# A planned attention-and-FFN kernel: filler matmuls in any free bank, a new identity and first-load order, v on VectorE only, SyncE holds in the planner, and a new instruction order

## The chip, the cores and the metric

The kernel runs on one core of a Trainium2 chip. The metric is the device time of one execution in microseconds (us), from the runs' timer. The profile's span runs from the first to the last instruction of one profiled execution; the timer shows a little more, for what lies around it.

## The reference

There are two stages. The first is linear attention with a "hedgehog" feature map, for 8 batches of 8 heads, 576 tokens, head width 64:

```
phi(x)  = [exp(p), exp(-p)]  with p = x @ w_phi - max|x @ w_phi|        (128 + 128 features)
kv      = sum over tokens of phi(k)^T v ;  z = sum over tokens of phi(k)
attn    = (phi(q) @ kv) / (phi(q) . z + 1e-6)
```

The second is a feed-forward network (FFN) on the 4608 tokens, laid out as 4608 x 512: `relu(x @ w_in)^2 @ w_out` with 2048 hidden units. Inputs and output are float32; the kernel's matmuls take bfloat16 and accumulate in float32.

## The kernel before

**Tiling.** A batch of attention has five groups of tokens: groups 0 to 3 hold 128-row blocks of two heads each, and group 4 holds the last 64 tokens of all heads (the "singles", tiles named `xks`, `xqs`, `xvs` below for their loads). For keys: a transpose gives `kT`; `project` (L598) or, in batch 0, L626, makes the projection in PSUM; VectorE takes the maximum (`mk`); ScalarE takes exp with both signs (`kp`, `kn`) and the exp of the maximum (`em_ops`); `v_ops` multiplies v by that factor into `va` (L720 for the singles, L724 for the rest); `kv_ops` (L741, L746) accumulates `kv`. For queries: `qmax_ops` and `q_ops` project twice (L774 or L598 for the maximum, L816 for the features), ScalarE makes `qp` and `qn`, and `out_ops` (L846) multiplies by `kv`, with a VectorE rescale between the two signs (L858), a reciprocal (L866) and the division (L870) into `xo`. `xo` is transposed into `xT`, the FFN's input.

**Transposes.** Batches 0 and 1 (`PE_IN`) transpose k and q on TensorE (L569) and copy the result out of PSUM; lists `CK`, `CQ`, `CK1`, `CQ1` say on VectorE or ScalarE. Batches 2 to 7 use DMA transposes issued by SyncE (SP), L582, one for k and one for q in a batch, each 18 blocks; `xo` goes through SP too from batch 1 on (L908).

**FFN.** The FFN runs in 9 chunks of 512 tokens, one batch behind attention (`ffn_in_small` L1003 for chunk 0, `ffn_in` L992, `ffn_out` L1057, `last_out` L1021), followed by ReLU on ScalarE (L972), the square on VectorE (L978), and stores from three `ot` buffers by SP (L1074). Chunk 8 collects the singles of all batches.

**Loads.** All loads of q, k, v and both weights go through the GpSimd (POOL) queue, cast on the way, at most eight in flight. `w_phi` comes in two halves through SP (L433).

**The order.** It is written out by a planner. `plan.add` records every operation with an engine, a cost (occupancy, latency), a key (due time) and what it reads and writes. `Machine.run` then simulates the engines: an engine that is free takes the available operation with the smallest key, subject to free PSUM banks (`place`, `fit`, `LIM`), and to two modes of TensorE ("tiled" projections with 64-row weights and the rest; a change of mode has a price). Keys are the list `KEYS`; `RELEASES` gives the earliest time of each load from batch 2 on, and `pin` makes such a load wait for the ScalarE instruction that the plan shows as finished by then (its "gate"). Each engine's program is then in plan order, and each engine executes strictly in its order.

**Planned DMA.** The planner has one DMA queue for SP and one for POOL. `SLACK` adds time to a landing by its class ("first" for the first two batches' loads and the weights, "ld" for later loads, "x" for transposes of `xo`, "kq" for those of k and q); `SHARE` is SP's part when both queues have work.

**Filler.** [...] the last loop of the kernel puts matmuls on a tile of zeros (`warm`, L1144) into each planned idle stretch of TensorE before `WARM_UP` = 23 us. They write PSUM bank 7, which the planner keeps free until then. The identity for TensorE's transposes is made on POOL by `make_identity` (a memset, then an `affine_select`), planned behind the first k load.

Of the kernel before, what the change touches and what calls it, by code (L numbers as in the profile page):

```python
# [22 lines left out]
SLACK = {"first": 0.4, "ld": 1.5, "x": 1.5, "kq": 2.5}  # L23
BEGIN = {"POOL": 1.25}
WARM_UP, COLD = 23.0, 6.0
# [14 lines left out]
class Op:  # L40
    __slots__ = ("eng", "occ", "lat", "key", "fn", "opens", "closes", "dma", "tiled", "release", "gate",
                 "succ", "n", "ready", "at", "seq", "what", "ins", "left", "done", "slack")

    def __init__(self, eng, cost, key, fn, opens, closes, dma, tiled, release, seq, what):
        self.eng, (self.occ, self.lat), self.key, self.fn = eng, cost, key, fn
        opens = () if opens is None else opens if isinstance(opens, tuple) else (opens,)
        self.opens, self.closes, self.dma, self.seq, self.what = opens, closes, dma, seq, what
        self.tiled, self.release, self.gate, self.ins = tiled, release, None, None
        self.succ, self.n, self.ready, self.at, self.done = {}, 0, 0.0, None, None
        self.slack = SLACK[dma[3]] if dma is not None and len(dma) > 3 else 0.0  # L50
# [48 lines left out]
class Machine:  # L99
# [5 lines left out]
    SHARE = {"x": 0.36, "st": 0.67, "ld": 0.5}  # L105

    def __init__(self, plan, limits, ahead, patience, want):
        self.plan, self.limits = plan, limits
        self.ahead, self.patience, self.want = ahead, patience, want
        self.free_at = [0.0] * (self.BANKS - 1) + [WARM_UP]  # L110
        self.open = {}
        self.q = {"SP": [], "POOL": []}
        self.q_t, self.q_v = 0.0, 0
        self.hist = {"SP": [], "POOL": []}
# [45 lines left out]
    def dma_advance(self, t):  # L160
        done = []
        while self.q_t < t - 1e-12:
            sp = self.speeds()
            step = t - self.q_t
            for k, l in self.q.items():
                if l:
                    step = min(step, l[0].left / sp[k])
            for k, l in self.q.items():
# [8 lines left out]
    def run(self):  # L177
# [28 lines left out]
        def dma_settle(t):  # L206
# [6 lines left out]
            sp = self.speeds()  # L213
            nxt = [self.q_t + l[0].left / sp[k] for k, l in self.q.items() if l]
            if nxt:
# [36 lines left out]
        while left:  # L252
# [12 lines left out]
            if e["free"] > t + 1e-9:  # L265
# [4 lines left out]
            while e["pending"] and e["pending"][0][0] <= t + 1e-9:  # L270
                bisect.insort(e["avail"], heapq.heappop(e["pending"])[2])
            op = pick(name, e, t)
# [8 lines left out]
            op.at = t  # L281
# [30 lines left out]
            if op.dma is not None:  # L312
                op.left = op.dma[0]
                self.hist[name].append(op)
# [8 lines left out]
def kernel(  # L323
# [107 lines left out]
    def f_wphi(half):  # L431
        def fn():
            pin(nc.sync.dma_start(out=wphi_f[half * 64 : half * 64 + 64, :], in_=w_phi))  # L433
        return fn

    for half in range(2):
        add("SP", (0.6, 0), -10, f_wphi(half), w=[("wphi_f", half)], dma=(0.3, HW_IN, "ld"), what="wphi")
# [8 lines left out]

    warmed = add("DVE", dve_cost(32), -1e4, f_warm, w=["warm"], what="warm")
# [102 lines left out]
    def attention(b):  # L550
# [157 lines left out]
        def v_ops(g0, g1, key):  # L708

            gs = [4] if g0 == 4 else list(range(g0, g1))  # L710
            for sg in range(2):
                on = K["CV"][2 * g0 + sg] if first else "DVE"
                ve = nc.vector if on == "DVE" else nc.gpsimd
                def fn(sg=sg, ve=ve):
                    t = va[s2][sg]
                    if g0 == 4:
# [3 lines left out]
                        pin(ve.tensor_tensor(  # L720
                            out=o[:, :, :, :D], in0=x, in1=o[:, :, :, D].to_broadcast([P, 4, 2, D]), op=ALU.mult))
                    else:
                        o = t[:, 8 * g0 : 8 * g1, :]
                        pin(ve.tensor_tensor(  # L724
# [3 lines left out]
                add(on, dve_cost(n) if on == "DVE" else (n / 500 + 0.1, n / 500 + 0.3), key, fn, r=of("xv", b, ["s"] if g0 == 4 else gs) + [("ve", s2, sg, g) for g in gs],  # L728
# [284 lines left out]
    def last_out(c, tt, part, key):  # L1013
# [26 lines left out]
        for half in range(2):  # L1040
            for u, (name, e) in enumerate((("SP", nc.sync), ("ACT", nc.scalar))):
# [4 lines left out]
                add(name, (0.5, 0.5), key + half, fn, r=[("otl", half)], what="stl")  # L1046
# [33 lines left out]
    def f_ident():  # L1080
        make_identity(nc, ident)

    add("POOL", (0.8, 1.0), -8.9, f_ident, w=["ident"], what="ident")
# [42 lines left out]
    warmed.key = -1e4  # L1126
# [9 lines left out]
    for op in order:  # L1136
        if op.eng == "PE" and op.at < WARM_UP:
            now[0] = filler
            n = 0
            while idle + (0.11 if idle < COLD else 0.058) < op.at - 0.03:  # L1140
                idle += 0.11 if idle < COLD else 0.058
                n += 1
            for _ in range(n):
                pin(nc.tensor.matmul(out=psum[:, 7, :P], lhsT=warm, rhs=warm, start=True, stop=True))  # L1144
# [21 lines left out]
    'CV': ['POOL', 'DVE', 'DVE', 'POOL', 'DVE', 'DVE', 'DVE', 'DVE', 'DVE', 'POOL'],  # L1166
    'KM': [1, 1, 1, 1, 1],
    'CK': ['DVE', 'ACT', 'ACT', 'DVE', 'DVE'],
    'CQ': ['DVE', 'DVE', 'DVE', 'ACT', 'ACT'],
    'CK1': ['ACT', 'ACT', 'ACT', 'ACT', 'DVE'],  # L1170
    'CQ1': ['DVE', 'DVE', 'DVE', 'DVE', 'DVE'],
# [4 lines left out]
    'LIM': {'tp': 6, 'b0': 7, 'att': 3, 'kv': 1, 'op': 2},  # L1176
    'AHEAD': 27.826,
    'PATIENCE': 5.762,
# [4 lines left out]
    -1188, 474, 253, 754, 1267, 528, 1719, 419, -2007, -2938, -2908, -2981, -4303, -4282, -3330, -3499, 919, 649,  # L1183
    1370, 2080, 1937, 1125, 1588, 1758, 2021, 2630, 1260, 2159, 2716, 4112, 2907, -2846, 3771, -1876, 4962, 4961,
    3120, 3409, 24214, 17442, 18795, 44151, 1509, 2174, 657, 972, 5105, 139, 1554, 1343, -8, 2664, 4605, 2242, 2239,
    1135, 1840, 5585, 430, 1295, 2238, 1136, 1707, 1336, 945, 443, 3793, 29611, 29873, 194, -588, 827, 594, 15584,
    776, 166, 14628, 305, 21064, 146, 1125, 885, 2743, 25589, -2180, 107, 907, 23181, 1452, 16457, 3036, 2675, 973,
    35728, 1936, 2335, 1747, 1866, 1305, 1774, 1112, 2112, 2270, 1379, 1304, 26789, 216, 26250, 17049, 1162, 2001,
    1665, 28376, 1869, 2852, 2457, 1250, 935, 1220, 2270, 1616, 1054, 10645, 20672, 2478, 1178, 2010, 999, 1923,
    393, 2483, 11257, 2804, 22023, 2533, 10980, 5031, 2532, 1743, 2463, 2204, 13503, 1506, 2348, 2785, 4142, 2901,  # L1190
    36176, 9646, 3718, 14023, 2255, 2290, 299, -72, 13807, 11062, 2403, 2778, 2102, 17466, 11387, 2050, 2319, 5032,
    14049, 8912, 1855, 14681, 1658, 2595, 25827, 3886, 3958, 10742, 18466, 4286, 7320, 4146, 26325, 2594, 9501,
    2696, 21621, -190, 22614, -1704, 2640, 35906, 4111, 22553, 3566, 6591, -314, 7751, 9572, 5930, 4224, 8630,
    14150, 14672, 4292, 7860, 4443, 2689, 2858, 7055, 3974, 4816, 6018, 2943, 13108, 2777, 2404, 33150, 35566, 3635,
    2965, 3806, 1699, 4189, 15290, 4266, 20860, 3962, 20258, 4549, 5477, 3203, 1892, 3524, 2854, 3813, 4795, 4887,
    4532, 5059, 6753, 20587, 26251, -357, 18509, -87, 3069, 5510, 31932, 1422, 6588, 5358, 6315, 1913, 4618, 24242,
    6773, 5370, 5986, 4151, 34128, 6057, 8183, 15483, 5660, 6078, 29747, 14492, 6266, 15335, 6540, 4409, 4759, -392,
    5661, 5347, 5290, 7491, 5505, 6298, 5763, 5960, 25044, 183, -812, 4467, 4387, 5327, 2497, 6865, 7116, 4719,
    6177, 5627, 6010, 6083, 6121, 6278, 4167, 24496, 7776, 8245, 6597, 6765, 29553, 5314, 11573, -110, 15484, 4913,
    6178, 8838, 19649, -231, 4916, 30701, 7786, 8322, 12085, 35149, 3500, 1077, 5339, 3084, -356, 3451, 3054, 17648,  # L1200
    2824, 2922, 16842, 5248, 3803, 2746, 14132, 5658, 17523, 29471, 5655, 3354, 4095, 4822, 5666, 4427, 5397, 3918,
    6360, 6495, 4759, 18063, 5919, 4532, 4501, 6236, 4423, 37527, 5746, 5835, 6510, 4027, 5065, 26396, 1751, 4806,
    5892, 9033, 5894, 4282, 5468, 5858, 1344, -3520, 3667, 24946, 25273, 25359, 3238, 4543, 4906, -95, 1079, 12985,
    7480, 10129, 2325, 37292, 53, 9165, 7565, 9657, 3425, 20459, 9576, 9725, 8791, 19377, 8125, 19178, 23716, 8786,
    -1952, 7595, 29986, 7634, 18755, 8663, 15981, 12146, 9487, 10448, 8819, 8908, 8691, -1929, 9521, 8863, 21811,
    9570, 10185, 7836, 11282, 9154, 7332, 37424, 7462, 7045, 6935, 6786, 9216, 9235, 19462, 10195, 11284, 8928,
    10835, 8511, 2871, 9295, 9783, 24159, 8664, 11351, 10113, 11142, 22190, 10398, 17777, 3185, 2391, -253, -948,
    11128, -2534, 425, 20649, 32343, 9102, 2944, 8733, 11654, 12476, 10197, 10427, 10530, 9734, 10615, 8748, -1123,
    10681, 6537, 10759, 12413, 12082, 32361, 14465, 3268, 11422, 11238, 11707, 11582, 23355, 12263, 11570, 4035,
    6591, 2840, 5604, 4489, 7936, 8602, 9080, 6114, 2760, 9508, 6016, 9010, 8259, 8506, -421, 6285, 7836, 7574,  # L1210
    8525, 9517, 18673, 7044, 6862, 7853, 13963, 7876, 8335, 5210, 5767, 7599, 8898, 29260, 5554, 5410, 8243, 9334,
    17403, 9243, 24144, 8353, 9108, 30600, 36971, 9137, 6764, 31407, 20905, 8686, 19278, 9290, 7237, 20576, 9945,
    9482, 9050, 10364, 27769, 11167, 8564, 5763, 4446, 10315, 8988, 16403, 4858, 9954, 6527, 11610, 7075, 5392,
    27034, 9410, 5480, -3552, 9698, 20309, 11741, 11397, 8887, 10295, 10825, 37395, 38223, 10882, 12346, 10736,
    9404, 12019, 9290, 228, 10345, 4314, 10319, 9622, 10045, 11538, 23123, 12591, 13084, 9699, 10200, 11107, 14578,
# [103 lines left out]
```

## Time and profile before

| | |
|---|---|
| median of 4 runs | 371.92 us (370.09 to 373.41) |
| the profiled execution's own time | 371.43 us |
| its span | 369.7 us, 8551 instructions |
| TensorE busy, VectorE, ScalarE, GpSimd | 350.4, 254.7, 267.5, 69.6 us |
| mean granted TensorE clock | 0.997 |
| bytes moved by DMA | 39.61 MB, 101478 packets |

How to read it: a matmul of 512 columns shows about 379 ns in the trace, but matmuls are pipelined, and successive ones start 216 ns apart (the starts in the trace). So busy time overstates what TensorE does. Where the text speaks of TensorE work in us, it counts matmuls at the distance of their starts: 216 ns for 512 columns, 56 ns for 128, 29 ns for 65, half of that for a tiled pair with 64-row weights. "Position 43 on TensorE" is a point of the program with 43 us of such work ahead of it; positions are counted in the instruction order as it is written out. In profile lines, a bracket gives the idle time of the engine before an instruction and what ended it; "SPq" and "POOLq" are the sequencers that issue DMAs.

### The profile page before, as it was taken

The numbers are of one execution on the slowest core, as the hardware profiler recorded it, in microseconds if no ns is written. First come the engines' busy times: TensorE is split into PE (matmuls) and PEld (weight loads), VectorE is DVE, ScalarE is ACT, GpSimd is POOL, SyncE is SP. The second block draws the span as 40 slices with busy tenths as digits, with TensorE's granted clock in tenths as the row PEclk, the third lists the DMA queues.
The fourth block names the chain that finished last, engine by engine and source line by source line (L and its number), as shares of the span: only waits on it lengthen the run. The fifth ranks groups of instructions, "written<-read, shape, count | busy, mean of one in ns | idle before, by whom it ended". The sixth has DMA issues, their size and how long they took to land.

```text
span 369.7 us, 8551 instructions
## 1 busy us (share of the span) xinstructions
PE 350.4 (95%) x3494; PEld 198.6 (54%) x3494; DVE 254.7 (69%) x426; ACT 267.5 (72%) x507; POOL 69.6 (19%) x99
## 2 busy tenths in 40 slices
PE   7977899978999999999999999999999999999994
PEld 7956778533564455545555445455454554444452
DVE  3997998768887977895787748888587750531500
ACT  3978998569959698898785977997787753723620
POOL 8795213001213320321003200013000000000000
PEclk9999999999999999999999999999999999999998
DMA  8999997971969798699929993158630032011023
GB/s 111 142 195 199 192 121 95 150 157 25 166 97 131 155 170 117 122 150 145 78 83 162 128 192 99 42 106 94 129 94 28 2 96 76 0 37 57 2 61 81
DMA packets 101478, 39.61 MB, mean 107 GB/s; under 512 B 76096, under 2 KB 96960, under 8 KB 101440
## 3 DMA queue, kind: packets, MB, share of 16 engines
q0 software_dynamic: 50592, 18.36, 46.2%
q1 hardware_dynamic: 50688, 20.59, 25.7%
q8 instruction: 27, 0.44, 0.5%
q10 hardware_dynamic: 160, 0.13, 0.1%
q14 instruction: 11, 0.09, 0.1%
HBM read 36.77 MB, written 9.44 MB: 125 GB/s over the span
## 4 chain that ended last, share of the span: by engine, by line
PE 57%; ACT 18%; DMA 9%; DVE 6%; issue 6%; POOL 2%; POOLq 0%; DVEq 0%; ACTq 0%
PE psum L992 22%; PE psum L1057 22%; ACT hr L972 4%; DMA xT<-xo 4%; PE psum L846 4%; ACT kp L684 3%; ACT kn L684 2%; DMA xk<-in_k_dram 2%; PE psum L741 2%; ACT qp L831 2%; PE psum L598 2%; DVE mq L781 2%; DMA kT<-xk 2%; PE psum L816 1%; ACT ot L1065 1%
## 5 line engine op out<-in xcount | busy, mean ns | idle before, releaser
L1057 PE MATMUL psum<-wout,h 128*128 128x512 bf16 x560 | 133.9, 379 | 0.5 <-ACT ot L1065 0.5
L992 PE MATMUL psum<-xT,win 128*128 128x512 bf16 x448 | 104.3, 379 | 4.5 <-DMA xT<-xo 2.6
L972 ACT ACTIVATE hr<-psum 128x512 bf16<-128x512 f32 x144 | 83.1, 608 | 29.3 <-PE psum L992 19.0
L978 DVE TENSOR_TENSOR h<-hr 128x512 bf16<-128x512 bf16 x144 | 58.9, 419 | 46.2 <-ACT hr L972 44.6
L992 PEld LDWEIGHTS <-win 128*128 128x128 bf16 x512 | 47.6, 98 | 61.1 <-issue 6.2
L1057 PEld LDWEIGHTS <-h 128*128 128x128 bf16 x560 | 50.2, 98 | 53.7 <-issue 2.3
L781 DVE TENSOR_REDUCE mq<-psum 128x8 f32<-128x1024 f32 (+1 forms) x40 | 43.9, 1111 | 9.1 <-PE psum L598 8.8
L831 ACT ACTIVATE qp<-psum 128x1024 bf16<-128x1024 f32 (+1 forms) x40 | 37.6, 944 | 10.0 <-PE psum L816 6.8
L1065 ACT ACTIVATE ot<-psum 128x512 f32<-128x512 f32 x35 | 21.1, 601 | 29.5 <-PE psum L1057 21.2
L724 DVE TENSOR_TENSOR va<-xv,va 128x1024 bf16<-128x1024 bf16 (+1 forms) x34 | 38.6, 1152 | 5.1 <-ACT va L703 5.1
L678 DVE TENSOR_REDUCE mk<-psum 128x8 f32<-128x1024 f32 (+1 forms) x35 | 38.0, 1108 | 3.8 <-PE psum L598 3.4
L858 DVE TENSOR_TENSOR psum<-psum,en 128x520 f32<-128x520 f32 (+1 forms) x40 | 27.6, 702 | 17.2 <-PE psum L846 11.8
L831 ACT ACTIVATE qn<-psum 128x1024 bf16<-128x1024 f32 (+1 forms) x40 | 37.6, 947 | 0.4 <-PE psum L846 0.4
L684 ACT ACTIVATE kp<-psum 128x1024 bf16<-128x1024 f32 (+1 forms) x35 | 32.8, 939 | 6.8 <-DVE mk L678 6.5
L684 ACT ACTIVATE kn<-psum 128x1024 bf16<-128x1024 f32 (+1 forms) x35 | 33.1, 945 | 0.1
L870 DVE TENSOR_TENSOR xo<-psum,rden 128x512 bf16<-128x512 f32 (+1 forms) x40 | 27.2, 685 | 1.0
L487 POOL DMA_DIRECT2D xq<-in_q_dram x16 | 14.2, 888 | 39.9 <-ACT va L703 13.8
L741 PE MATMUL psum<-va,kp 128*128 128x65 bf16 x256 | 19.9, 194 | 0.2 <-ACT kv L756 0.2
L476 POOL DMA_DIRECT2D xk<-in_k_dram x16 | 10.1, 630 | 53.0 <-DVE mq L781 19.7
L741 PE MATMUL psum<-va,kn 128*128 128x65 bf16 x256 | 19.9, 193 | 0.0
L741 PEld LDWEIGHTS <-kp 128*128 128x128 bf16 x256 | 17.4, 97 | 4.0 <-DVE va L724 0.9
L846 PEld LDWEIGHTS <-qp 128*128 128x128 bf16 x320 | 14.3, 97 | 8.9 <-issue 2.3
(67 smaller groups left out, 379.5 us busy)
## 6 DMA issues: line engine op xcount, KB each, us to landing
out_dram<-ot SPq DMA_DIRECT2D x32, 256.0 KB, 2.4
xv<-in_v_dram POOLq DMA_DIRECT2D x8, 512.0 KB, 7.8
xq<-in_q_dram POOLq DMA_DIRECT2D x16, 256.0 KB, 6.4
xk<-in_k_dram POOLq DMA_DIRECT2D x7, 512.0 KB, 7.1
win<-in_moe_w_in_dram POOLq DMA_DIRECT2D x4, 512.0 KB, 8.7
wout<-in_moe_w_out_dram POOLq DMA_DIRECT2D x4, 512.0 KB, 11.4
out_dram<-ot SPq DMA_DIRECT2D x6, 128.0 KB, 2.3
xk<-in_k_dram POOLq DMA_DIRECT2D x16, 32.0 KB, 4.9
```

Of the source, the lines that this page charges most:

```text
L678: pin(nc.vector.tensor_reduce(out=mk_view(g), in_=ps2(pj)[:, :, : n * Fd].rearrange("p e (i f) -> p e i f", f=Fd), axis=AX.X, op=ALU.max, ...
L684: pin(nc.scalar.activation(out=dst[slot][:, :, :n, :].rearrange("p e i f -> p e (i f)"), in_=ps2(pj)[:, :, : n * Fd], func=ACT.Exp, scale= ...
L724: pin(ve.tensor_tensor(out=o[:, :, :D], in0=xv[s2][:, 512 * g0 : 512 * g1].rearrange("p (m d) -> p m d", d=D), in1=o[:, :, D].to_broadcast ...
L741: pin(nc.tensor.matmul(out=o[:, sg, hi, :], lhsT=(kp, kn)[sg][kgroup[pr]][:, j % 2, 2 * hi + j // 2, :], rhs=va[s2][sg_of(sg, pr)][:, 8 * ...
L781: pin(nc.vector.tensor_reduce(out=mqb[:, c, :, :n], in_=ps2(pj)[:, :, : n * Fd].rearrange("p e (i f) -> p e i f", f=Fd), axis=AX.X, op=ALU ...
L831: pin(nc.scalar.activation(out=o, in_=i_, func=ACT.Exp, scale=sgn))
L846: pin(nc.tensor.matmul(out=o[:, u // 4, u % 4 * D1 : (u % 4 + 1) * D1], lhsT=(qp, qn)[sg][slot][:, u * m : u * m + P], rhs=kv_sb[s2][:, h ...
L858: pin(nc.vector.tensor_tensor(out=o, in0=o, in1=enb[:m, c, :].rearrange("t (b h) -> t b h", b=2).to_broadcast([m, 2, 4, D1]), op=ALU.mult))
L972: pin(nc.scalar.activation(out=hr[sl], in_=ps1(g), func=ACT.Relu))
L978: pin(nc.vector.tensor_tensor(out=dst, in0=i_, in1=i_, op=ALU.mult))
L992: pin(nc.tensor.matmul(out=o, lhsT=win[mc // 4][:, kc, mc % 4 * P : (mc % 4 + 1) * P], rhs=x, start=(kc == 0), stop=(kc == KC - 1)))
L1057: pin(nc.tensor.matmul(out=ps1(g), lhsT=h2[c % 2][mc // 4][:, mc % 4, tt * P : (tt + 1) * P], rhs=wout[mc // 4][:, mc % 4, :], start=(mc = ...
```

## The change

1. **Filler.** `WARM_UP` rises from 23 to 45, bank 7 is no longer kept free, and a filler matmul goes into any bank that the plan shows as free when TensorE falls idle (`op.spare`); where none is free there is no filler.
2. **Start.** The identity is a VectorE memset of zero (`f_ident0`) and one `affine_select` on POOL; `make_identity` is gone. In the new order the select stands behind three loads on POOL; the first k load is now the one of two head pairs (256 KB), then one pair. The second half of `w_phi` is issued by ScalarE.
3. **v.** `CV` is gone: all of batch 0's `v_ops` run on VectorE. Three of the ten were on POOL.
4. **SP holds.** A DMA transpose of k or q (`held`) keeps the planned SP busy until no more than `RING` = 1.05 us of it is left to move. This is in the plan only; it adds no instruction.
5. **Other constants of the plan**: `SLACK`, `SHARE["st"]`, `LIM`, `AHEAD`, `PATIENCE`, the cost of the last store, and the engines of the PSUM copies of batches 0 and 1.
6. **Order**: new `KEYS` and `RELEASES`.

```diff
-SLACK = {"first": 0.4, "ld": 1.5, "x": 1.5, "kq": 2.5}
+SLACK = {"first": 1.2, "ld": 1.5, "x": 1.5, "kq": 1.5}
+
+RING = 1.05
 BEGIN = {"POOL": 1.25}
-WARM_UP, COLD = 23.0, 6.0
+WARM_UP, COLD = 45.0, 6.0
...
+        self.held = dma is not None and len(dma) > 3 and dma[3] == "kq"
...
-    SHARE = {"x": 0.36, "st": 0.67, "ld": 0.5}
+    SHARE = {"x": 0.36, "st": 0.35, "ld": 0.5}
...
-        self.free_at = [0.0] * (self.BANKS - 1) + [WARM_UP]
+        self.free_at = [0.0] * self.BANKS
+        self.holding = None
...
+            h = self.holding
+            if h is not None and h.left <= RING + 1e-9:
+                self.holding = None
+                engines["SP"]["free"] = max(engines["SP"]["free"], self.q_t)
+                post(engines["SP"]["free"], "SP")
+                h = None
...
-            if e["free"] > t + 1e-9:
+            if e["free"] > t + 1e-9 or name == "SP" and self.holding is not None:
                 continue
...
+            spare = next((b for b in range(self.BANKS) if self.free_at[b] <= e["free"] + 1e-9), None) if name == "PE" else None
...
-    for half in range(2):
-        add("SP", (0.6, 0), -10, f_wphi(half), w=[("wphi_f", half)], dma=(0.3, HW_IN, "ld"), what="wphi")
+    first_ops = []
+    for half, (name, e) in enumerate((("SP", nc.sync), ("ACT", nc.scalar))):
+        def fn(half=half, e=e):
+            pin(e.dma_start(out=wphi_f[half * 64 : half * 64 + 64, :], in_=w_phi))
+        first_ops.append(add(name, (0.6, 2.2), -10, fn, w=[("wphi_f", half)], what="wphi"))
...
+    def f_ident0():
+        pin(nc.vector.memset(ident, 0.0))
+
+    cleared = add("DVE", (0.12, 0.25), -9e3, f_ident0, w=["ident0"], what="ident0")
...
-                on = K["CV"][2 * g0 + sg] if first else "DVE"
-                ve = nc.vector if on == "DVE" else nc.gpsimd
-                def fn(sg=sg, ve=ve):
+                def fn(sg=sg):
...
-        make_identity(nc, ident)
-
-    add("POOL", (0.8, 1.0), -8.9, f_ident, w=["ident"], what="ident")
+        pin(nc.gpsimd.affine_select(out=ident, in_=ident, compare_op=ALU.not_equal, fill=1.0, base=0,
+                                    pattern=[[-1, P]], channel_multiplier=1))
+
+    add("POOL", (0.45, 0.6), -8.9, f_ident, r=["ident0"], w=["ident"], what="ident")
...
-            while idle + (0.11 if idle < COLD else 0.058) < op.at - 0.03:
+            while op.spare is not None and idle + (0.11 if idle < COLD else 0.058) < op.at - 0.03:
...
-                pin(nc.tensor.matmul(out=psum[:, 7, :P], lhsT=warm, rhs=warm, start=True, stop=True))
+                pin(nc.tensor.matmul(out=psum[:, op.spare, :P], lhsT=warm, rhs=warm, start=True, stop=True))
...
-    'CV': ['POOL', 'DVE', 'DVE', 'POOL', 'DVE', 'DVE', 'DVE', 'DVE', 'DVE', 'POOL'],
-    'CK': ['DVE', 'ACT', 'ACT', 'DVE', 'DVE'],
-    'CQ': ['DVE', 'DVE', 'DVE', 'ACT', 'ACT'],
-    'CK1': ['ACT', 'ACT', 'ACT', 'ACT', 'DVE'],
-    'CQ1': ['DVE', 'DVE', 'DVE', 'DVE', 'DVE'],
+    'CK': ['DVE', 'ACT', 'DVE', 'DVE', 'ACT'],
+    'CQ': ['DVE', 'DVE', 'ACT', 'ACT', 'ACT'],
+    'CK1': ['ACT', 'ACT', 'DVE', 'ACT', 'DVE'],
+    'CQ1': ['ACT', 'ACT', 'DVE', 'DVE', 'DVE'],
...
-    'LIM': {'tp': 6, 'b0': 7, 'att': 3, 'kv': 1, 'op': 2},
-    'AHEAD': 27.826,
-    'PATIENCE': 5.762,
+    'LIM': {'tp': 3, 'att': 3, 'kv': 1, 'hp': 6, 'op': 2},
+    'AHEAD': 250.08,
+    'PATIENCE': 3.491,
...
```

In the order as written out, the fillers go from 170 to 158 matmuls. Those before the first k transpose go from 33 to 51; 29 stand further down the program than any did before (position 4.9 and on). Six groups of fillers now wait for ScalarE or VectorE to finish with the bank that they write; before, none did. The changes of TensorE's mode go from 120 to 116. Some operations stand as follows:

| position on TensorE | before | after |
|---|---|---|
| batch 2: k load, main part | 34.3 | 7.7 |
| batch 2: k load, second half of the singles | 38.3 | 20.5 |
| batch 2: q transpose on SP | 36.1 | 36.9 |
| batch 2: k transpose on SP | 42.7 | 32.0 |
| batch 2: first projection of k | 49.7 | 45.8 |
| batch 2: first use of transposed q | 47.3 | 43.1 |
| FFN chunk 1: last `xo` transpose on SP, then first matmul | 47.8, 51.3 | 47.1, 52.1 |

Before, the q transpose of batch 2 is ahead of its k transpose on SP; after, behind it.

## The prediction

> **What bounds the kernel now.** First the page: who is busy, and when.
>
> ```profile
> PE 350.4 (95%) x3494; PEld 198.6 (54%) x3494; DVE 254.7 (69%) x426; ACT 267.5 (72%) x507; POOL 69.6 (19%) x99
> ...
> PE   7977899978999999999999999999999999999994
> ...
> PEclk9999999999999999999999999999999999999998
> DMA  8999997971969798699929993158630032011023
> ```
>
> TensorE looks full from slice 6 on, but busy is not work. At the distances of their starts the real matmuls add up to 315.5 us and the fillers to 9.5 us; the first starts at 1.0 and the last at 364.5 us. So 38.5 us are lost between starts: 12.7 before 30 us, then 0.8 per 10 us in an ordinary stretch (mean of 100 to 200 us), and 4.7 from 70 to 90 us. The end is set by TensorE's order; a change gains only what shortens those losses. The clock is granted nearly everywhere, so fillers have little to win. DMA is near full to 80 us.
>
> Next the busy time by stretch (busy us of PE, PEld, DVE, ACT, POOL; clock; DMA share; GB/s), to see who limits the start:
>
> ```profile
> 10.00:20.00 10.00, 9.97 (x177) 8.79 (x176) 9.92 (x17) 9.83 (x30) 8.03 (x11) 1.00 1.32 142
> 20.00:30.00 10.00, 6.54 (x116) 4.81 (x113) 8.16 (x11) 7.31 (x17) 7.03 (x9) 1.00 1.36 201
> ...
> 40.00:50.00 10.00, 9.04 (x165) 8.52 (x165) 9.33 (x19) 9.97 (x18) 2.12 (x3) 1.00 1.40 178
> ```
>
> VectorE and ScalarE are full there, TensorE waits for them. Last the chain that ended last, for the worst loss (start, us, what):
>
> ```profile
> 60.36 0.89 POOL xk L468
> 61.24 2.21 issue
> 63.46 8.33 DMA xk<-in_k_dram
> 71.79 0.02 issue
> 71.81 6.18 DMA kT<-xk
> 77.99 0.03 issue
> 78.02 3.61 DMA xT<-xo
> ```
>
> Batch 2's k is loaded too late; its transpose and, behind it on SP, an `xo` transpose land at 78.0 and 81.6. The starts of matmuls show the price: gaps of 1.09 us at 76.7 (first k projection), 1.64 at 79.8 (FFN chunk 1) and 1.29 at 87.3, 4.0 together.
>
> **What the Trainium skill says.** "TensorE: Matmul & The Clock Gate", Part 1: the array starts at half clock, rises after a busy window of about 3.4 us and falls after an idle one. The trace agrees: fillers start 107 ns apart at 6.2 to 7.6 us, 55 ns at 8.9 us, and gaps up to 2 us cost no clock later. "GPSIMD Engine Reference", section 8: GpSimd shares SBUF interfaces with VectorE and is about half as fast on elementwise work. The trace agrees (1.05 to 1.45 against 0.69 us; VectorE beside it takes 1.56). "DMA: Bandwidth & Descriptors", "Anatomy of one DMA": a semaphore wait happens on the issuing sequencer, so it holds what is queued behind; "Issuing engines are not separate DMA queues": SP's and POOL's DMAs interleave on the same engines. The trace agrees: the q transpose issued at 61.79 beside loads kept SP for 7.20 us and landed 10.2 us later; that issued at 218.1, with no load running, kept it 2.7 and landed after 4.7.
>
> ```profile
> 61.79 7.20 SPq L582 DMA_TRANSPOSE qT<-xq  x1
> ...
> 71.81 3.48 SPq L582 DMA_TRANSPOSE kT<-xk  x1
> 75.34 3.88 SPq L908 DMA_TRANSPOSE xT<-xo  x3
> ```
>
> **The change part by part.** The sum is made against the profiled execution, 371.43 us (span 369.7 and 1.7 around it); the median of the runs, 371.92, is 0.5 above.
>
> *Order of batch 2.* From the k load (or its last half of singles) to the first projection there were 11.4 us of TensorE work (38.3 to 49.7); now 25.3 (20.5 to 45.8). The bytes ahead of it in POOL's queue: up to its last singles 8448 KB; before, 8480 KB had landed at 53.8 us. So it lands near 54, and the transpose, at position 32 (near 58 us), need not wait. At 6.2 us it lands by 65, against use near 74. The q transpose then follows 4.9 us behind on the same queue, with 6.2 us to its use; alone it takes 4.7, beside loads 10.2. By then the loads needed early are in, so I take about 6 and a small remainder. What is late next is VectorE and ScalarE: from 80 to 100 us ScalarE is busy 19.1 of 20. Of the 4.7 lost from 70 to 90, 1.7 is ordinary; I take the rest, -3.0, with ends at -4.0 (all three gaps) and -1.0 (q takes the place of k).
>
> The loads moved back for it: `wout0` stands behind 6848 KB and should land near 45 us (before: 6784 at 44.5), its use at position 23.6 is near 46; the first v load of batch 1 should land near 50 (7904 KB at 50.3 before), use near 52. Tight, taken as nothing; if that cover is gone, 1 to 2 us each.
>
> *Start.* These two rows (start, us, engine) and the wait in brackets are what the new identity removes:
>
> ```profile
> 5.46 0.31 POOL masks.py:199 TENSOR_SCALAR_AFFINE_SELECT ident<-ident 128x128 bf16<-128x128 bf16 x1
> ...
> 5.82 0.58 PE L569 MATMUL psum<-ident,xk 128*128 128x128 bf16 x4 [1.13 <-POOL ident masks.py:199]
> ```
>
> The identity will be ready near 4.3 us (three load issues, 1.25 to 3.7, then the select). But the first load is now 256 KB: 128 KB landed at 4.7 and the next 256 KB at 6.4, so 256 KB land near 5.5. And 51 fillers at 107 ns run from 1.0 to 6.45 (or near 5.9, if the clock rises meanwhile). First transpose 5.5 to 6.45 against 5.82: no gain by itself, but twice as much k comes with it, and VectorE can make its two first copies (0.8 us) before its maxima instead of between them. `w_phi`: VectorE casts it at 4.43, its first user runs at 7.51; and the issue of 0.6 us on ScalarE stands before an idle of 4.4 us: nothing. If that cover went, 0.6.
>
> *v.* Three v products go to VectorE: 3 x 0.69 = +2.07. The two that ran beside POOL fall from 1.56 and 1.54 to 0.69: -1.72. POOL's queue loses 3.6 us of compute in front of its later load issues, which mostly wait for a landing anyway: nothing. One copy less on VectorE in the q part (-0.4), one of batch 1 more before the first rescale (+0.3). VectorE's chain to the first rescale: 0.35 - 0.8 - 0.4 + 0.3 = -0.55; ends -1.5 (the whole identity wait) and +1.0 (fillers hold the transposes).
>
> *Fillers.* No clock to win: 0.003 of 370 is 1.1 us, all in the first and last stretch. New are six groups that wait for a reader of their bank. The reader is at most a ScalarE exp of 1024 columns, 1.02 us, and behind the filler stand, in order, the kv product and the batch-0 outputs that lead to the first FFN matmul (33.1 us before). Below nothing is excluded, since nothing else waits less for them. Ends 0 and 6.1; the plan picks a bank that it thinks read, so I take +0.5.
>
> *Mode changes.* 116 instead of 120; the starts show 96 ns into and 121 out of the tiled mode: -0.4.
>
> *Copies moved to ScalarE.* At positions 40 to 60 ScalarE has done about 2 us more than before, at position 100 the same. Nothing, with an end of +2, since it is full from 40 to 50.
>
> *Other FFN starts.* Before, chunks 2, 3, 4 lost 0.9, 0.5, 1.0 us there, their transposes landing in 4.5 to 7.3 us beside 512 KB loads, against 2.3 alone. Now chunks 3 and 4 have only small loads or later ones beside them; but batch 4's k has 14.4 us from load to use where it had 16.5, and its q 13.6 where it had 17.6. I take -0.3, from -2 to +2.
>
> *SP holds* and the constants add no instruction.
>
> Sum: -3.0 - 0.55 + 0.5 - 0.4 - 0.3 = -3.75, so 371.43 - 3.75 = 367.7.
>
> **The rivals.** *Everything fits* (the plan now knows SP's hold): k's 4.0, the start's 1.5, 0.4 and 2 of FFN starts, 371.43 - 7.9 = 363.5. For it: each loss has a visible cause. Against: orders of this length always leave new waits.
>
> *The stall is hidden anyway.* With k early, ScalarE and VectorE, 2 us of work richer at that point, are the next bound, and only about 1 us comes out: 370.5. For it: 19.1 of 20 busy from 80 to 100. Against: part of that is the backlog of the stall itself.
>
> *Slower: the bank waits of the fillers.* TensorE stands in order behind a zero matmul that waits for ScalarE, so the chain to the first FFN matmul is drawn out by each wait; the six cost their full 1.02, and k gives 1.0: 371.43 + 6.1 - 1.0 = 376.5. It decides from 3.75 us of such waits on. For it: ScalarE is full in that stretch. Against: TensorE idles there in any case (6.4 us lost from 20 to 30), which covers waits shorter than that.
>
> **How the numbers follow.** Forecast 0.45, everything fits 0.14, hidden 0.21, slower 0.20. The forecast's own range is 365 to 370.3. About 1%, 3.7 us, is what a measurement of this kernel can tell from no change: faster means below 368.2, which is all of "fits" and some six tenths of the forecast (0.42); slower means above 375.6, most of the last case (0.17); the rest is 0.41. The range reaches into both outer cases, 363 to 376.
>
> **What would show it.** k right: no chain piece of a k load between 60 and 82 us, no gap above 1 us at the first k projection of batch 2 and at FFN chunk 1. Start right: no wait for the identity, and the first FFN matmul no later than 33.1. v right: every batch-0 v product near 0.69 us. Fillers harmless: no filler row with an idle of more than 0.3 us before it. The forecast is wrong if q's transpose of batch 2 lands after 73 us, if a weight lands after its place in the order, or if fillers wait for ScalarE near a microsecond each.

## The result and the profile after

The changed kernel takes 372.86 us (median of 44 runs, 369.19 to 376.23), the kernel before 371.68 (63 runs). The ratio is 1.0014, with a 95% interval from 0.9998 to 1.003: no change that can be measured, where the forecast was -3.75 us. Medians are of all runs; a ratio leaves out the runs more than 1.5% above the fastest of their kernel, so it can differ from the quotient of the medians. The profiled execution took 373.84 us with a span of 371.8.

The page of the changed kernel, with busy times, then TensorE, its clock and DMA in 40 slices:

```profile
PE 354.2 (95%) x3482; PEld 199.9 (54%) x3482; DVE 253.7 (68%) x428; ACT 268.5 (72%) x509; POOL 66.2 (18%) x95
...
PE   8599999979999799999999999999999999999994
...
PEclk9959999999999989999999999999999999999998
DMA  8999999898669986998896298735261022001113
```

Two things are new. The clock has a hole in its third slice (5, where there was 9) and a dent in the fifteenth. And the weak slices of TensorE have moved: before, the third to the fifth, the ninth and the tenth; now the second (9 to 19 us), the ninth (74 to 84) and the fourteenth (121 to 130).

The busy time by stretch (PE, PEld, DVE, ACT, POOL; granted clock; DMA share; GB/s) shows the hole:

```profile
10.00:20.00 10.00, 5.35 (x62) 3.46 (x60) 7.78 (x15) 7.85 (x25) 5.48 (x8) 0.89 1.52 189
18.00:28.00 10.00, 9.59 (x97) 7.24 (x96) 6.88 (x10) 7.93 (x17) 5.74 (x8) 0.50 1.42 160
```

From 18 to 28 us every matmul runs at half clock. Ahead of that TensorE stood still for 2.3 us at 10.1 us (its 44 fillers, meant for that place, had started at 7.7 and were used up), and from 15 to 18 us for 0.7, 1.0 and 1.1 us, with no filler at all: the plan shows no free bank when TensorE falls idle there (the last of these gaps lies inside one operation, where no filler can stand). The kernel before had 6.0 us of fillers between 10 and 20 us, the changed one 1.4. The first FFN matmul comes at 35.9 us; it came at 33.1.

SyncE's queue (start, us, instruction) shows that batch 2's k does what was forecast:

```profile
53.31 2.82 SPq L599 DMA_TRANSPOSE kT<-xk  x1
56.35 6.04 SPq L599 DMA_TRANSPOSE qT<-xq  x1
...
68.86 4.20 SPq L923 DMA_TRANSPOSE xT<-xo  x2
```

The transposes of k and q are issued one behind the other and land at 59.8 and 67.2 us, ahead of their uses. No piece of a k load is left in the chain between 60 and 82 us. But the chain now has this in the same place:

```profile
68.14 0.69 DVE xo L885
68.83 0.03 DVE psum L873
68.86 7.35 DMA xT<-xo
76.20 0.03 issue
76.23 0.02 DVEq L885
76.25 0.04 issue
76.30 0.69 DVE xo L885
```

VectorE waits until the buffer that it wrote at 68.14 has been transposed. SyncE issues that transpose at 68.86, 0.03 us after the write has ended, and it lands at 76.20, after 7.35 us: beside it runs batch 3's load of v (512 KB, issued at 68.84; in the kernel before at 96.6). TensorE waits behind VectorE for the bank. Their rows in the timeline (start, us, instruction, idle before it):

```profile
76.30 0.69 DVE L885 TENSOR_TENSOR xo<-psum,rden 128x512 bf16<-128x512 f32 x1 [2.80 <-DMA xT<-xo]
...
77.04 0.28 PE L831 MATMUL psum<-qT,wphi 64*128 64x256 bf16 x2 [1.81 <-DVE xo L885]
```

`xo` has three buffers, and only two are in use at that moment: between 68.14 and 76.30 there is one other write, at 71.14. The kernel hands out the buffers in turn while it records its operations (`xs = xslot[0] % 3`), and the planner then puts the writes in another order, in which this one takes the same buffer as the last but one.

And later there is a second wait of that kind, on the three `ot` buffers from which SyncE stores:

```profile
123.05 0.50 ACT ot L1080
123.56 5.51 DMA out_dram<-ot
129.11 0.04 issue
129.16 0.61 ACT ot L1080
```

ScalarE waits for the store of the buffer that it wrote just before, which takes 5.51 us to land; the other two, written at 106.8 and 117.2, are free by then. TensorE waits for ScalarE (2.42 us in the timeline at 129.8), and behind it the clock falls again: 0.56 from 130 to 133 us.

### The profile page after: what moved, and what is told of

The parts are those of the page before. It is cut to its first block, busy times and chain, and to the rows that moved or that the text cites. A ratio compares the mean times of both kernels' runs of the same rounds, so it can differ in the third digit from the quotient of the medians.

```text
span 371.8 us, 8526 instructions
## 1 busy us (share of the span) xinstructions
PE 354.2 (95%) x3482; PEld 199.9 (54%) x3482; DVE 253.7 (68%) x428; ACT 268.5 (72%) x509; POOL 66.2 (18%) x95
## 4 chain that ended last, share of the span: by engine, by line
PE 73%; ACT 10%; DVE 7%; DMA 6%; issue 1%; POOL 0%; DVEq 0%; ACTq 0%; POOLq 0%
PE psum L1072 29%; PE psum L1007 24%; PE psum L861 5%; PE psum L756 4%; PE psum L615 3%; ACT hr L987 3%; DMA xv<-in_v_dram 2%; PE psum L831 2%; DMA xT<-xo 2%; PE psum L1018 2%; ACT kp L701 2%; ACT kn L701 2%; DVE mq L796 2%; DMA out_dram<-ot 1%; DVE va L739 1%
## 5 line engine op out<-in xcount | busy, mean ns | idle before, releaser
L1007 PE MATMUL psum<-xT,win 128*128 128x512 bf16 x448 | 105.8, 384 | 2.4 <-ACT ot L1080 2.4
L987 ACT ACTIVATE hr<-psum 128x512 bf16<-128x512 f32 x144 | 82.0, 603 | 30.2 <-PE psum L1007 22.6
L756 PE MATMUL psum<-va,kp 128*128 128x65 bf16 x256 | 21.2, 199 | 0.1
L756 PE MATMUL psum<-va,kn 128*128 128x65 bf16 x256 | 21.1, 198 | 0.0
L756 PEld LDWEIGHTS <-kp 128*128 128x128 bf16 x256 | 18.4, 101 | 3.6 <-issue 1.1
L756 PEld LDWEIGHTS <-kn 128*128 128x128 bf16 x256 | 17.9, 101 | 1.7 <-ACT kn L701 0.2
```

The lines of the kernel that those rows point to most:

```text
L756: pin(nc.tensor.matmul(out=o[:, sg, hi, :], lhsT=(kp, kn)[sg][kgroup[pr]][:, j % 2, 2 * hi + j // 2, :], rhs=va[s2][sg_of(sg, pr)][:, 8 * ...
L987: pin(nc.scalar.activation(out=hr[sl], in_=ps1(g), func=ACT.Relu))
L1007: pin(nc.tensor.matmul(out=o, lhsT=win[mc // 4][:, kc, mc % 4 * P : (mc % 4 + 1) * P], rhs=x, start=(kc == 0), stop=(kc == KC - 1)))
```

## The experiments

Three theories, numbered 1 to 3 in the expectations. *Clock*: the start loses its gain because fillers are missing where TensorE idles. *Start*: loads and VectorE make the start late, and the clock is a symptom. *Rings* (a ring is a set of buffers used in turn): the k load's gain went into waits for `xo` and `ot` buffers. The expectations say that SyncE holds the transposes and stores behind these; the lines above show both issued 0.03 us after the write, so it is their landing that takes the time. Every edit below leaves the order of the plan as it was, unless it says otherwise; ratios are to the kernel before, with the 95% interval.

### Fillers taken away

In the kernel before, no filler from 10 us of the plan on (115 of 170 go); the same edit in the changed kernel (102 of 158; its expectation counts 98) is the second run.

```diff
-        if op.eng == "PE" and op.at < WARM_UP:
+        if op.eng == "PE" and op.at < 10.0:
```

> The kernel before with its own plan, and without the zero matmuls that stand after 10 us of the plan (6.0 us of TensorE time between 10 and 20 us); nothing else moves. Theory 1 (missing fillers cost clock): the granted clock falls below 0.9 in at least one 10-us stretch before 40 us, real TensorE work stands 2 to 4 us later at 30 us than in the kernel before, and the median is 1.5 to 4 us above it (ratio 1.004 to 1.011). Theory 2 (the changed kernel's start is late because of its loads and its VectorE work, the clock is a symptom): the clock may fall, but the work waits for data anyway; the median stays within 0.8 us of the kernel before. The forecast's own step, that the clock holds nothing to win, says the same as theory 2.

> The changed kernel with its plan, and without every zero matmul after 10 us of the plan (the 98 that stand at 7.7 us and later). Theory 1: the clock falls earlier, already in the stretch from 10 to 20 us, and the median rises by 0.5 to 3 us above the changed kernel. Rival (the late fillers delay TensorE by the banks they wait for, as the slower rival of the forecast had it): the median falls by 0.5 us or more. Theory 2: within 0.5 us of the changed kernel.

The kernel before becomes slower by 1.27%: 376.11 us, ratio 1.0127 (1.0091 to 1.0162). Its stretches:

```profile
10.00:20.00 10.00, 5.13 (x60) 3.57 (x61) 9.40 (x14) 9.71 (x30) 8.46 (x12) 0.70 1.35 147
20.00:30.00 10.00, 7.31 (x86) 5.00 (x86) 8.09 (x9) 5.09 (x12) 6.12 (x8) 0.62 1.37 199
```

The clock falls to 0.70 and 0.62, where it was 1.00 and 1.00, and the first ReLU on ScalarE starts 2.0 us later. So fillers do hold the clock of the kernel before, and are worth some 4.7 us there, a little more than theory 1 expected.

The time of the changed kernel does not show it: 372.69 us, 1.0014 (0.9991 to 1.0037), the ratio that it has with them. Its clock does:

```profile
10.00:20.00 10.00, 4.21 (x28) 2.03 (x29) 7.12 (x15) 7.44 (x23) 5.18 (x8) 0.60 1.49 186
```

It had 0.89 there with the fillers. In the profiles, half clock now lasts from 11.9 to 29.0 us, where it lasted from 17.8 to 28.0. So the late fillers hold some clock, as theory 1 had it, but taking them away does not cost the 0.5 to 3 us that it expected. They do not delay the kernel either, as the forecast's slower rival had it. Theory 2 named the size, within 0.5 us. They stand beside the gaps, and the clock falls in any case.

### Fillers added

In the changed kernel, 84 more, by the place of the operation on TensorE (bank, number): 38 behind the 44 at 7.7 us; 32 at 15 us, into bank 7, which comes free shortly after TensorE falls idle; 14 at 17.3 us. In the kernel before, 34 more in its gap at 20.5 us.

```diff
...
+            more = {6: (0, 38), 12: (7, 32), 13: (0, 14)}.get(nth)
+            nth += 1
+            if more is not None:
+                op.spare, n = more[0], n + more[1]
             for _ in range(n):
```

> The changed kernel with its plan and 84 zero matmuls more in three places where its TensorE stood still: 38 at 10.3 us, 32 at 15 us in a bank that comes free at the beginning of that gap, 14 at 17.3 us. Theory 1: the granted clock stays at 0.95 or more from 18 to 28 us, where the changed kernel had 0.50, real work stands 1.5 to 3 us earlier at 30 us than in the changed kernel, and the median is 1 to 3 us lower (369.9 to 371.9 if the changed kernel is at 372.9). Theory 2: clock up, median within 0.7 us of the changed kernel. If the fillers wait for their bank, 0 to 1 us is lost at 15 us.

> The kernel before with 34 zero matmuls more in its one gap of 2 us between 10 and 25 us of time (at 20.5 us, where TensorE waits for the second half of batch 0's q). Theory 1: the wait itself stays, but the clock can't fall behind it, as it did in one profile of this start (0.83 from 20 to 30 us, 1.6 us lost); as the kernel before loses that in some of its executions only, the median is 0 to 1.5 us lower (ratio 0.996 to 1.000). If the zero matmuls delay the transposes behind them, the ratio is above 1.001.

The changed kernel with 84 more, by stretch:

```profile
10.00:20.00 10.00, 9.46 (x155) 8.07 (x153) 7.84 (x15) 8.21 (x25) 6.08 (x9) 1.00 1.53 191
18.00:28.00 10.00, 9.77 (x164) 7.08 (x163) 8.98 (x12) 9.03 (x22) 6.25 (x9) 1.00 1.39 153
```

The clock is 1.00 throughout; in the profile the first ReLU starts 3.6 us earlier than in the changed kernel, and 0.8 earlier than in the kernel before. So the clock is a cause: the *start* theory doesn't hold for the profiled executions. In time these are no typical ones: the profile with more fillers took 368.87 us, the lowest of its 22 runs, and that of the changed kernel 373.84, 1.0 above its median. In clock they are: the mean granted clock of a run is 0.988 to 1.000 with the added fillers and 0.975 to 0.991 in the 44 runs of the changed kernel. The median is 371.57 us, ratio 0.9994 (0.997 to 1.0017), 0.0020 below the changed kernel with about 0.003 of uncertainty: some 0.7 us (1.3 by the medians), which these runs can't tell from nothing. So it is shown that these fillers bring back the clock, and not that they bring back time. In the kernel before, 0.9998 (0.9971 to 1.0025): nothing; its profile keeps the clock behind the filled gap and loses it from 31.0 to 34.4 us. The first expectation was right on the clock; its gain of 1 to 3 us is not shown. The gaps at 71.3 (1.98) and 123.5 us (2.38) are still there.

### Longer rings

In the changed kernel with the added fillers, `xo` gets four buffers for three, and `ot` four (the fourth shares the tile of the last stores, `otl`). The planner still counts three, so the order is the same; but which write takes which buffer changes with the number.

```diff
-    xo = ring("xo", 3, [8 * D])
+    xo = ring("xo", 4, [8 * D])
...
-    ot = ring("ot", 3, [DM], F32)
-    otl = sb("otl", [DM], F32)
+    ot = ring("ot", 4, [DM], F32)
+    otl = ot[3]
...
             xs = xslot[0] % 3
+            xr = xslot[0] % 4
...
             sl = oslot[0] % 3
+            so = oslot[0] % 4
...
```

> The changed kernel with the 84 zero matmuls more of the run before it, and with longer rings: xo of four buffers in place of three, and the output tile ot of four in place of three (the fourth one shares the room of the tile for the last stores). The order of the work is the same. Theory 3 (the k load's gain went into waits for the transposes and stores that SyncE holds): the gaps at 71.3 us (1.98 us, xo waits for a transpose of xo) and 123.5 us (2.38 us, ot waits for a store) fall below 0.7 us each, and the median is 2 to 4 us below the run without longer rings: a ratio to the kernel before of 0.988 to 0.994. Rival (those buffers were late only because TensorE's other work was): another wait takes their place and the ratio stays at 0.997 or more.

> The same with the longer ring of xo alone. Theory 3: the gap at 71 us shrinks from 1.98 to below 0.7 us, the one at 123 us stays between 2.0 and 2.8 us, and the ratio to the kernel before lies 0.002 to 0.005 below that of the run without longer rings (0.9994). Rival: no more than 0.5 us (0.0013).

> The same with the longer ring of ot alone. Theory 3: the gap at 123 us shrinks from 2.38 to below 0.7 us, the one at 71 us stays near 2.0 us, and the ratio to the kernel before lies 0.003 to 0.007 below 0.9994, more than the gap itself where the clock falls after the gap. Rival: no more than 0.5 us.

| | median us | ratio | interval |
|---|---|---|---|
| added fillers alone | 371.57 | 0.9994 | 0.997 to 1.0017 |
| and `xo` of four | 368.38 | 0.9912 | 0.989 to 0.9935 |
| and `ot` of four | 370.35 | 0.9921 | 0.9892 to 0.9949 |
| and both | 365.44 | 0.9854 | 0.9812 to 0.9897 |

`xo` gives 0.0082 (0.9994 - 0.9912), 3.0 us, `ot` 0.0073, 2.7 us, both 0.0140, 5.2 us: they add up, within 0.003 to 0.005 of uncertainty, and each is a little more than expected. By the quotients of the medians, `xo` gives 3.4 us, `ot` 1.4 and both 6.3, so the price of `ot` alone is not settled. In the profiles, with `xo` of four the first gap is gone and the second stays (2.53 us); with `ot` of four the second is gone, but the first is 0.84 us and not the 2.0 expected, so that run may hold a part of the other's gain. With both, the page reads

```profile
PE   8999999999999999999999999999999999999994
...
PEclk9999999999999999999999999999999999999998
```

and TensorE goes through the place where it stood still without a pause:

```profile
71.78 0.38 PE L1073 MATMUL psum<-wout,h 128*128 128x512 bf16 x1
72.09 0.28 PE L831 MATMUL psum<-qT,wphi 64*128 64x256 bf16 x2
```

This version beats both kernels, by 1.5%.

So these waits cost about 5 us, and this edit takes them away. That it needs a fourth buffer is not shown. For `ot` two of three were free when ScalarE waited; handed out in the order of the writes, three would have done there. For `xo`, by the times above, the write at 77.13 would then have waited for the landing at 76.20, an estimated gain of 0.8 us. This was not tried.

### The same rings without the fillers, and in the kernel before

> The changed kernel with the longer rings alone (xo four, ot four), without zero matmuls added. If the two losses are separate and add up: the start still loses its clock (0.5 to 0.8 from 18 to 28 us), the gaps at 75 and 127 us are gone, and the ratio to the kernel before is that of the changed kernel (1.0014) less what the rings gave beside the added zero matmuls (0.014): 0.985 to 0.991, about 0.002 above the run with both. If the rings only pay when the start is early, the ratio stays above 0.995.

> The kernel before, its order untouched, with the same longer rings. If those waits belong to the changed kernel's order alone (in the kernel before, the chain of 60 to 90 us runs through the k load and its transpose), the ratio is 0.997 to 1.001. If both orders pay for short rings, it is below 0.994, and the changed order has no part in the gain.

The changed kernel with the rings alone: 366.7 us, 0.9863 (0.9828 to 0.9898), though its clock is 0.67 from 20 to 30 us. The kernel before with the rings: 371.75 us, 1.0006 (0.9984 to 1.0027). The list of waits says why it differs (who, for what: us in all, times, longest). In the kernel before:

```profile
ACT ot L1065 <- DMA out_dram<-ot: 8.0, 3, 4.4
```

In the changed kernel:

```profile
ACT ot L1080 <- DMA out_dram<-ot: 5.3, 2, 2.8
DVE xo L885 <- DMA xT<-xo: 2.8, 1, 2.8
```

The kernel before never waits for an `xo` buffer. It waits longer for `ot` in all, but 7.2 of the 8.0 us lie after 300 us, and their removal brought nothing that shows; only 0.8 lies before 200 us. In the changed kernel 2.8 of them hit TensorE at 123 us. With the longer rings, the kernel before gets a wait that it did not have:

```profile
DVE xo L871 <- DMA xT<-xo: 1.8, 1, 1.8
```

It lies at 184.4 us, where the write takes the buffer of the write just before it, and TensorE stands still for 1.44 us. So the number of buffers does not decide alone. The two waits of the changed kernel belong to its order. Between two kernels that both have the long rings, the change is worth 0.9863 / 1.0006 = 0.9857, or 5.3 us (1.0% to 1.8%), of which up to 1.4 may be this new wait.

### The earlier k alone, in the old order

Batch 2's v load moves behind its k loads on POOL, and the k loads take over v's gate.

```diff
...
+    k2 = [o for o in k2 if order.index(o) > order.index(v2)]
+    for o in k2:
+        o.gate = v2.gate
+    order.remove(v2)
+    order.insert(order.index(max(k2, key=order.index)) + 1, v2)
```

> The kernel before with one change in the order of its loads: batch 2's k (512 KB and one 32 KB piece) is issued ahead of batch 2's v (512 KB), as in the changed kernel, with the wait of the load that it takes the place of; the order of TensorE, VectorE, ScalarE and SyncE is that of the kernel before. The forecast priced an earlier k at -3.0 us (ends -4.0 and -1.0). If that step is right on its own: k's last piece lands before 68 us instead of 71.8, the gaps at 76.7, 79.8 and 87.3 us (1.1, 1.6 and 1.3 us) close, and the median is 2 to 4 us lower. Theory 3 (another transfer or ring takes the place of the wait removed): the gaps at 76 to 88 us shrink by 2 us or more, and at most 1 us of it is left at the end.

> The kernel before with batch 2's k loaded ahead of its v and with the longer rings. Without them the earlier k cost 0.8% (ratio 1.0079), with a gap of 2.57 us at 75.7 us that waits for xo and a transpose of 6.5 us. Theory 3: the fourth xo buffer takes that gap away, and what the forecast priced for the earlier k (-3.0 us) appears: ratio 0.989 to 0.996, at least 0.003 below that of the longer rings alone. Rival (the load of v, moved into the time of the transposes, slows them whatever the rings are): ratio 1.000 or more.

Alone it is slower: 373.83 us, 1.0079 (1.0054 to 1.0104). SyncE's queue:

```profile
63.15 7.99 SPq L582 DMA_TRANSPOSE qT<-xq  x1
71.19 2.09 SPq L908 DMA_TRANSPOSE xT<-xo  x1
73.33 0.58 SPq L1074 DMA_DIRECT2D out_dram<-ot  x1
74.07 4.16 SPq L582 DMA_TRANSPOSE kT<-xk  x1
```

k is in place at 70.9 us (issued at 60.8 and 61.6, at most 9.2 to land), and yet its transpose is issued later than before (74.07 against 71.81), because it stands behind q's transpose on SyncE, and that one, with v's 512 KB now beside it, held the queue to 71.1 us and landed after 12.6 us (10.2 before). The transpose of `xo` waits there too: written by 68.0 us, it is issued at 71.19 and takes 6.49 more to land. So a wait like that of the changed kernel appears in the old order, here with SyncE's hold in it: `xo` waits 3.4 us for a buffer, TensorE 2.41. Neither guess for this run came true. In the kernel before two waits ended together there: k landed at 71.8 us, and q's transpose at 72.0. With the longer rings the ratio is 1.0058 (1.0034 to 1.0082), 0.005 above the rings alone: the rival of that expectation was right, the theory wrong. The run brings k forward by 0.9 us only; the changed kernel issues the main load at 30.8 us, where it was 60.4. It also issues k's transpose before batch 2's load of v (53.31 against 56.02 us) and q's 0.3 us behind it. An early load without these is therefore not tested, and which part brings the gain at batch 2 stays open.

### v on VectorE alone

In the kernel before, all of batch 0's products on VectorE:

```diff
                 ve = nc.vector if on == "DVE" else nc.gpsimd
+                ve = nc.vector
```

> The kernel before with the three products of v that GpSimd computes in batch 0 moved to VectorE, at the places where the order has them (3 x 0.68 us more on VectorE, which is busy 9.9 of the 10 us from 10 to 20 us). The forecast's step for the start and v took -0.55 us for both together, with ends -1.5 and +1.0. If VectorE sets the start, the products delay what stands behind them there: 0.7 to 2 us later at 34 us and a ratio of 1.002 to 1.005. If the products on GpSimd (and the loads behind them) set it, 0 to 1.5 us earlier and a ratio of 0.996 to 1.000.

370.65 us, 0.997 (0.9951 to 0.9989): 1.1 us gained, as the second guess had it, and inside the ends of the forecast's step.

Not tried: the new identity and first load alone, the changed kernel with bank 7 kept free, and three buffers handed out in the order of the writes.

## Why the prediction was wrong

**The gain was there, and the two waits that took its place were not in the sum.** With long rings in both kernels, the change gives -5.3 us (up to 1.4 of it the old order's new wait), at least the -3.75 of the sum. With three buffers each, `xo` (3.0 us) and `ot` (2.7 us) give it back: -5.3 + 5.7 = +0.4, against +0.5 measured (0.0014 of 372). The prices of the two rings come from the kernel with added fillers; that they hold together without them is borne out by the run with rings alone (0.9863). How the 5.3 us divide among the parts of the change is not shown; *v* alone gave 1.1 in the kernel before.

**The step that failed first: "What is late next is VectorE and ScalarE."** The step on batch 2 had k's and q's transposes in time: k's is issued at 53.3 us and lands at 59.8 (forecast near 58 and by 65), q's lands at 67.2, before 73, though after 10.8 us and not the "about 6" taken for it. For what is late next it looked at busy engines, and not at the buffers between VectorE and SyncE. `xo`'s chain was in view: the chain of the kernel before ends in `DMA xT<-xo`, the text names "an `xo` transpose" behind k on SyncE. What wasn't asked is which `xo` buffer each write takes in the new order, and how long the transpose that reads it takes to land beside the loads that the order puts there: 7.35 us, where those of 60 to 90 us in the kernel before took 2.4 to 3.6. The 1.98 us gap is the place where most of the -3.0 went.

**The second: "Other FFN starts", -0.3 with an end of +2.** The store wait of 123 us falls here: +2.7 (1.4 by the medians). The step looked at transposes beside loads, and not at stores: this one took 5.51 us to land, and the next write of `ot` takes its buffer.

**The third: "No clock to win", "fillers have little to win".** It asked only what more clock there was to gain, with the clock at 0.997. The fillers that held it between 10 and 20 us were worth 4.7 us in the kernel before, and the change takes away 4.6 of their 6.0 us. The start should have come 0.55 us earlier; in the profile the first ReLU came 2.8 us later, and 0.8 earlier once the clock was held. What it costs at the median is less and isn't settled: 0.7 us, and between -0.3 and 1.8 by the intervals; with the longer rings, where the profile without added fillers has lost the clock too, the two medians are 1.3 us apart. By the Trainium skill, "TensorE: Matmul & The Clock Gate", Part 1, the gate looks at windows that run freely, and whether a gap costs clock then depends on where it falls in a window. The profiles agree: the start of the kernel before is the same program up to 50 us in its own profile and in the one with the earlier k, and its clock from 20 to 30 us was 1.00 in one and 0.83 in the other.

**Right:** *v* (batch 0's products at 0.64 to 0.69 us; -1.1 us alone). *Fillers' bank waits*: the timeline shows no idle before any filler from 2 to 36 us, so +0.5 was too much. *The start's wait for the identity* is gone (first transpose at 5.59 against 5.82), though the first FFN matmul came at 35.9, not by the 33.1 that the forecast named.

**The rivals.** "Slower: the bank waits" fell with those waits: the timeline shows none, and the run without late fillers is no faster. "The stall is hidden anyway" named the size (370.5) nearest to the result, but not by its reason: ScalarE, "the next bound", was not, since two more buffers bring 5 us at the same ScalarE time. With the longer rings alone the order takes 366.7 us, near the 367.7 of the sum; "Everything fits" (363.5) is not reached even with fillers added (365.44). That the sum's size comes out there is in part luck, since it had neither the rings nor the clock in it. The measured time lies inside the range, at a place that the sum gave no reason for.

## What to carry to other kernels

Where a change moves transfers, look at each ring of buffers that a DMA empties: which write takes which buffer in the new order, and how long the DMA that reads it takes to land beside its new neighbours. A ring that was never waited for can be the next stall, even with a buffer free, where the buffers are numbered in another order than that of the work. Read a filler by the gap it stands in, not by the mean clock: a clock of 0.997 may be the work of the fillers that a change takes away. And before giving up on an order that brings nothing, list its longest waits for a buffer: here one buffer more in each of two rings turned 0 into 1.4%.

## What was not expected of the hardware

Gaps of 0.7, 1.0 and 1.1 us within 3.2 us, after one of 2.3 us at 10 us, were followed by 10 us at half clock (18 to 28 us, 0.50). From 20 us on TensorE shows no idle, and still stays at half clock until 28.0 us:

```profile
20.00:30.00 10.00, 10.00 (x126) 7.74 (x123) 6.18 (x8) 6.62 (x15) 5.13 (x7) 0.60 1.32 165
```

The same page of the Trainium skill gives a busy window of about 3.4 us as enough for the full clock, and an idle one of that length as what takes it away (it also tells of a kernel whose frequent short idles made the clock swing, without their lengths); here it took 8 us of work until it came back, and it fell with no single gap above 2.3 us. The length of a window is in the traces: apart from the start and the very end, half clock lasts 3.4 us or a multiple of it in every profile that shows it (3.4 at 130.4 us in the changed kernel, 10.2 at 17.8; 13.7 and 17.1 in the kernel before and the changed one with fillers taken away). In the kernel before, the gap of 2.0 us at 20.5 us was followed by half clock in one profile and not in the other, so the forecast's reading that gaps up to 2 us cost no clock holds for its own profile only.
